# A dilated convolution with gates: the order of its first loads, and its doubled and halved weights

## The chip, the cores and the metric

The kernel runs on one core of one Trainium2 chip. The metric is the device time of one execution in microseconds (us); the median of several runs counts. A profiled execution of the same kernel gives the trace. In it the engines are PE (TensorE, matrix products; PEld its weight loads), DVE (VectorE), ACT (ScalarE), POOL (GpSimd) and SP (SyncE, which here only issues transfers).

## The reference

x has 2 batches of 16,000 steps with 256 channels, w three taps of 256 x 512, w_o 256 x 256, all bf16. The steps of the taps lie two apart and look backwards.

```python
B, T, D = x.shape
K = w.shape[0]
dil = 2
pad = (K - 1) * dil
xp = jnp.pad(x, ((0, 0), (pad, 0), (0, 0)))
h = jnp.einsum('btc,cd->btd', xp[:, pad:pad + T, :], w[0])
for i in range(1, K):
    off = pad - i * dil
    h = h + jnp.einsum('btc,cd->btd', xp[:, off:off + T, :], w[i])
f = h[..., :D].copy()
g = h[..., D:].copy()
z = jnp.tanh(f) * _sigmoid(g)
return z @ w_o
```

## The kernel before

**Tiling.** Four consecutive steps are one row; a group is up to 256 rows (1,024 steps), and the columns of a tile are rows. `xt` holds x transposed, channels on the partitions: `[128, 4, 2, rows]`, the 4 being the place in a row, the 2 the halves of the channels. `views` gives four views of it: `xc` and `yc` are places 0, 1 and 2, 3 of a row, `xp` and `yp` the same of the row before. The 512 output channels of the convolution are four blocks of 128, taken in `O_ORDER` (0, 2, 1, 3); blocks 0 and 1 go through tanh, 2 and 3 through sigmoid. A step k of the main loop is one block of one group, k = 4 x group + place in that order.

**Two ways to compute a block.** Group 0 (160 rows) is computed directly (`direct`, L236): for each tap two products (halves of the channels) into bank a (places 0, 1) and two into bank b (places 2, 3), in the order `TAPS`; for bank a, taps 0, 1, 2 read `xc`, `yp`, `xp`, for bank b `yc`, `xc`, `yp`. All later groups use four products instead of six (`products`, L217): `mm` = `xc` - `yp` with the weights `wm`, `pp` = `xc` + `yp` with `wp`, and the differences `dd` with tap 0 or tap 2. `wp` and `wm` are half of (tap 0 + tap 2) plus or minus half of tap 1 (`weights`, L141 to L144: ScalarE halves tap 1 into `wh_sb`, VectorE makes `wt_sb`, `wm_sb`, `wp_sb`). `copy_m2` (L247, ScalarE) copies the product of `mm` from bank b into `ss`; `combine` (L254, L255, VectorE) makes b = a - ss and a = a + ss; then the products of `dd` are added into both banks, and `activate` (L268, ScalarE) reads them. `gate` (L282, L286, VectorE) multiplies tanh and sigmoid, `out_mm` (L307) multiplies by w_o, `out_evict` (L326) copies the result out, and SyncE stores it.

**Queues and order.** The order on each engine is written out by hand; an engine runs its instructions in program order. Banks a and b have three buffers each, `ps_o` two. GpSimd makes most of `dd` (L192).

**Start.** VectorE clears `warm`, and TensorE runs `N_WARM[0]` = 27 products with it (L92). SyncE issues the load of x for group 0 (`xn`, L122, 320 KB), tap 0 (`w0_sb`, L126, 256 KB), the transposing load of chunk 1 (L105), `wo_sb` (L131, 128 KB) and the transposing load of chunk 2. A chunk is one group (chunks 0 and 1) or two. ScalarE issues taps 1 and 2 in one transfer (L118, 512 KB) beside its table load (L117). Chunk 0 isn't transposed by a transfer: `turn` (L155 to L163) does it on TensorE, 16 transposes, of whose four copies out of PSUM VectorE makes those for places 0, 1 (L161) and ScalarE those for places 2, 3 (L163). Six more products with `warm` follow, then the direct products of blocks k = 0, 1, 2, tap by tap. Then come the weights, `activate` for these three blocks, `pre_m` and `pre_p` for group 1 and its `dd`. The fourth block of group 0 (k = 3) and the first of group 1 (k = 4, `N_DIRECT`) are interleaved:

```python
direct(3, TAPS[:-1])
products(N_DIRECT, 2)
products(N_DIRECT, 1)
copy_m2(N_DIRECT)
direct(3, TAPS[-1:])
```

where 2 stands for `mm` with `wm`, 1 for `pp` with `wp`. The trace names all tap tiles `w_sb`.

Of the kernel before, what the change touches and what calls it, by code (L numbers as in the profile page):

```python
# [8 lines left out]
ACT = mybir.ActivationFunctionType  # L9
ALU = mybir.AluOpType  # L10
# [3 lines left out]
def kernel(  # L14
# [15 lines left out]

    nc = tc.nc
    bf16 = mybir.dt.bfloat16
    f32 = mybir.dt.float32
    B, T, D = x.shape
    K, _, D2 = w.shape
    P = 128
    assert K == 3 and D % P == 0 and D2 == 2 * D and T % 64 == 0
    CT = D // P  # L40
    NT = D // P
    RH = 16
    RG = 256
    N_WARM = (27, 6)
    O_ORDER = (0, 2, 1, 3)
    TAPS = (1, 2, 0)
    FIRST = (160,)
    LAST = (128, 128)
    TILES = ((0, 80), (80, 80))
    N_DIRECT = 4  # L50

    def sizes(first, last):
        rem = T // 4 - sum(first) - sum(last)
        assert rem >= 0
        odd = [rem % RG] if rem % RG else []
        return list(first) + [RG] * (rem // RG) + odd + list(last)
# [2 lines left out]
    groups, chunks = [], []  # L59
    for b in range(B):  # L60
        r0 = 0
        rs = sizes(FIRST if b == 0 else (), LAST if b == B - 1 else ())
        cuts = [1, 1] if b == 0 else []
        i = 0
        while i < len(rs):
            n = cuts.pop(0) if cuts else 2
            part = rs[i:i + n]
            chunks.append((b, r0, sum(part), len(groups), len(part)))
            for r in part:
                groups.append(dict(b=b, r0=r0, R=r, chunk=len(chunks) - 1, col=r0 - chunks[-1][1]))  # L70
                r0 += r
            i += n
    XW = max(c[2] for c in chunks)

    consts = ctx.enter_context(tc.tile_pool(name="consts", bufs=1))
# [13 lines left out]
    def warm_up(n):  # L89
        wps = ps_a.tile([P, 2 * RG], f32, name="a")  # L90
        for _ in range(n):
            nc.tensor.matmul(wps[:, :P], lhsT=warm[:], rhs=warm[:], start=True, stop=True)  # L92

    xts = {}

    def load_chunk(c):
# [13 lines left out]

    warm = consts.tile([P, P], bf16)
    nc.vector.memset(warm[:], 0.0)
    w0_sb = consts.tile([P, CT, D2], bf16)
    w12_sb = consts.tile([P, 2, CT, D2], bf16)
    wo_sb = consts.tile([P, NT, D], bf16)
    w_taps = [w0_sb, w12_sb[:, 0], w12_sb[:, 1]]
    nc.scalar.preload_act_table(ACT.Sigmoid)  # L117
    nc.scalar.dma_start(out=w12_sb[:], in_=w[1:3].rearrange("k (ct c) d -> c k ct d", c=P))  # L118
    warm_up(N_WARM[0])
    nx, rx = len(TILES), TILES[0][1]  # L120
    xn = consts.tile([P, nx, 4, D], bf16, name="xn")
    nc.sync.dma_start(  # L122
        out=xn[:rx], in_=x[0, 0:4 * nx * rx, :].rearrange("(i r j) c -> r i j c", i=nx, j=4)
    )
    xns = [xn[:, i] for i in range(nx)]
    nc.sync.dma_start(out=w0_sb[:], in_=w[0].rearrange("(ct c) d -> c ct d", c=P))  # L126
    ident = consts.tile([P, P], bf16)
    make_identity(nc, ident[:])
    for c in range(2):
        load_chunk(c)  # L130
    nc.sync.dma_start(out=wo_sb[:], in_=w_o.rearrange("(ct c) d -> c ct d", c=P))  # L131
    load_chunk(2)
    loaded = 3

    wh_sb = consts.tile([P, CT, D2], bf16)
    wt_sb = consts.tile([P, CT, D2], f32)
    wp_sb = consts.tile([P, CT, D2], bf16)
    wm_sb = consts.tile([P, CT, D2], bf16)

    def weights():  # L140
        nc.scalar.mul(wh_sb[:], w_taps[1], 0.5)  # L141
        nc.vector.tensor_tensor(out=wt_sb[:], in0=w_taps[0][:], in1=w_taps[2], op=ALU.add)
        for dst, op in ((wm_sb, ALU.subtract), (wp_sb, ALU.add)):
            nc.vector.scalar_tensor_tensor(  # L144
                out=dst[:], in0=wt_sb[:], scalar=0.5, in1=wh_sb[:], op0=ALU.mult, op1=op,
            )

    def turn(i):
        r0, r = TILES[i]
        for h in range(2):  # L150
            pool, tag = ((ps_o, "o_ps"), (ps_b, "b"))[i]
            tp = pool.tile([P, 2, CT, P], bf16, name="tp", tag=tag)
            for j in range(2):
                for ct in range(CT):
                    nc.tensor.transpose(  # L155
                        out=tp[:, j, ct, :r], in_=xns[i][:r, 2 * h + j, ct * P:(ct + 1) * P],
                        identity=ident[:r, :r],
                    )
            dst = xts[0][:, 2 * h:2 * h + 2, :, RH + r0:RH + r0 + r]
            if h == 0:  # L160
                nc.vector.tensor_copy(out=dst, in_=tp[:, :, :, :r])  # L161
            else:
                nc.scalar.copy(out=dst, in_=tp[:, :, :, :r])  # L163
# [7 lines left out]
    def pre_m(g):  # L171
        xp, yp, xc, yc = views(g)
        G = groups[g]
        G["m"] = m_pool.tile([P, 2, CT, RG], bf16, name="mm")
        return nc.vector.tensor_tensor(out=G["m"][:, :, :, :G["R"]], in0=xc, in1=yp, op=ALU.subtract)  # L175

    def pre_p(g):
        xp, yp, xc, yc = views(g)
        G = groups[g]
        G["p"] = p_pool.tile([P, 2, CT, RG], bf16, name="pp")  # L180
        return nc.vector.tensor_tensor(out=G["p"][:, :, :, :G["R"]], in0=xc, in1=yp, op=ALU.add)  # L181
# [19 lines left out]
    def products(k, which):  # L201
        g, oi = divmod(k, 4)
        G = groups[g]
        o = O_ORDER[oi]
        osl = slice(o * P, (o + 1) * P)
        R = G["R"]
        N = 2 * R
        if which in (1, 2):
            G["ab"[which - 1], oi] = (ps_a, ps_b)[which - 1].tile([P, 2 * RG], f32, name="ab"[which - 1])
        wmat, mv, bank, first = {  # L210
            2: (wm_sb, lambda ct: G["m"][:, :, ct, :R], "b", True),
            1: (wp_sb, lambda ct: G["p"][:, :, ct, :R], "a", True),
            3: (w_taps[0], lambda ct: G["d"][:, 2:4, ct, :R], "b", False),
            0: (w_taps[2], lambda ct: G["d"][:, 0:2, ct, :R], "a", False),
        }[which]
        for ct in range(CT):
            nc.tensor.matmul(  # L217
                G[bank, oi][:, :N], lhsT=wmat[:, ct, osl], rhs=mv(ct),
                start=first and ct == 0, stop=ct == CT - 1, skip_group_check=True,
            )  # L220

    def direct(k, taps):

        g, oi = divmod(k, 4)
        G = groups[g]
        o = O_ORDER[oi]
        osl = slice(o * P, (o + 1) * P)
        R = G["R"]
        xp, yp, xc, yc = views(g)
        for tap in taps:  # L230
            if tap == TAPS[0]:
                G["a", oi] = ps_a.tile([P, 2 * RG], f32, name="a")
                G["b", oi] = ps_b.tile([P, 2 * RG], f32, name="b")
            for bank, mv in (("a", (xc, yp, xp)[tap]), ("b", (yc, xc, yp)[tap])):
                for ct in range(CT):
                    nc.tensor.matmul(  # L236
                        G[bank, oi][:, :2 * R], lhsT=w_taps[tap][:, ct, osl], rhs=mv[:, :, ct, :],
                        start=tap == TAPS[0] and ct == 0, stop=tap == TAPS[-1] and ct == CT - 1,
                        skip_group_check=True,
                    )  # L240
# [16 lines left out]
    def activate(k):  # L257
        g, oi = divmod(k, 4)
        G = groups[g]
        R = G["R"]  # L260
        o = O_ORDER[oi]
        if oi == 0:
            G["th"] = act_pool.tile([P, NT, 4, RG], bf16, name="th")
            G["sg"] = act_pool.tile([P, NT, 4, RG], bf16, name="sg")
            G["z"] = z_pool.tile([P, NT, 4, RG], bf16, name="zz")
        dst = G["th"][:, o] if o < NT else G["sg"][:, o - NT]
        for h, bank in ((1, "b"), (0, "a")):
            nc.scalar.activation(  # L268
                out=dst[:, 2 * h:2 * h + 2, :R],
                in_=G[bank, oi][:, :2 * R].rearrange("p (q r) -> p q r", q=2),  # L270
                func=ACT.Tanh if o < NT else ACT.Sigmoid,
            )

    def gate(g, dt):
# [100 lines left out]
    todo, made = [], []  # L375
    turn(0)
    turn(1)
    warm_up(N_WARM[1])
    for tap in TAPS:
        for k in range(3):  # L380
            direct(k, (tap,))
    weights()
    for k in range(3):
        activate(k)
    pre_m(1)
    pre_p(1)
    for part in range(3):
        last = pre_d(1, part, nc.vector)
    pre_d(1, 3, nc.gpsimd, last)

    direct(3, TAPS[:-1])
    products(N_DIRECT, 2)
    products(N_DIRECT, 1)
    copy_m2(N_DIRECT)
    direct(3, TAPS[-1:])
    activate(3)
    combine(N_DIRECT)
    gate(0, 0)
    drain(0, N_DIRECT + 2, gate(0, 1))

    k = N_DIRECT + 1
    while k <= NB:
        g, oi = divmod(k, 4)
# [20 lines left out]
        last = None  # L424
        if k < NB and oi == (1 if g == 1 else 0) and g + 1 < NG:
            last = pre_m(g + 1)
        elif k < NB and oi == 2 and g + 1 < NG:
            last = pre_p(g + 1)
        elif oi == 3 and g < NG:
            last = gate(g, 0)  # L430
        elif oi == 1 and 1 < g < NG:
            last = gate(g - 1, 1)
# [42 lines left out]
```

## Time and profile before

| | us |
|---|---|
| Median of 3 runs | 285.53 |
| Lowest and highest | 285.46, 285.62 |
| The profiled execution | 285.54 |
| Span of its instructions | 283.6 |
| Issue of x, and time to landing | 0.74, 3.8 |
| Issue of taps 1 and 2, and time to landing | 0.76, 5.1 |
| Issue of tap 0, and time to landing | 1.20, 5.5 |
| First direct product | 5.99 |
| First product of the sums and differences (`wm`) | 12.00 |
| Granted TensorE clock, mean | 1.000 |

The times of instructions are counted from the start of the span; the time of an execution has 1.9 us around the span. A row of the timeline has the start, the duration, engine, line, operation, and tiles written and read; rows that follow each other are merged (x2, x27), and square brackets tell how long the engine was idle before, and what ended that. One product's duration has its way through the array in it, so that products in a row overlap: their pitch, from start to start, is shorter. "To landing" runs from the start of the issue until the whole transfer has been reported.

### The profile page before, as it was taken

To read this page: it belongs to the slowest core of one execution; us is meant where nothing else is said; L and a number is where in the kernel's file an instruction comes from. 1 tells how busy PE (TensorE), PEld (TensorE's weight loads), DVE (VectorE), ACT (ScalarE), POOL (GpSimd) and SP (SyncE) were. 2 spreads that over 40 slices of the span, in tenths; PEclk is the share of its full clock that TensorE was granted. 3 is DMA by queue.
4 is the path that set the end of the run, shared out by engine and by line. 5 is a ranking of instruction groups with operands and counts; after the bars stand their busy time and mean duration, and the time that the engine had idled before them with its cause. 6 is when DMAs were issued, how large, how long until landed. Compare 5 with 4: busy or idle time off the path is not lost.

```text
span 283.6 us, 4821 instructions
## 1 busy us (share of the span) xinstructions
PE 278.1 (98%) x1621; PEld 157.0 (55%) x1621; DVE 240.7 (85%) x403; ACT 260.3 (92%) x521; POOL 126.3 (45%) x133
## 2 busy tenths in 40 slices
PE   7999999999999999999999999999999999999994
PEld 6645555555555555555555555555555555555783
DVE  1999888888888888888888888888888888888884
ACT  4489999999999999999999999999999999999994
POOL 1145454445445544544554455445445544543430
PEclk9999999999999999999999999999999999999999
DMA  7964691732828228091461814528282341401232
GB/s 202 207 153 104 164 198 74 169 97 85 180 74 191 75 83 216 37 226 66 118 158 46 220 74 107 160 74 192 75 181 85 89 124 60 119 37 75 76 113 81
DMA packets 76039, 34.50 MB, mean 122 GB/s; under 512 B 66512, under 2 KB 68048, under 8 KB 76016
## 3 DMA queue, kind: packets, MB, share of 16 engines
q1 hardware_dynamic: 75488, 33.69, 45.1%
q10 hardware_dynamic: 528, 0.52, 0.6%
q8 instruction: 12, 0.20, 0.3%
q14 instruction: 11, 0.09, 0.1%
HBM read 1.25 MB, written 16.38 MB: 62 GB/s over the span
## 4 chain that ended last, share of the span: by engine, by line
PE 96%; DMA 2%; DVE 0%; DVEq 0%; issue 0%; ACT 0%
PE a L217 37%; PE b L217 37%; PE o_ps L307 19%; DMA w_sb<-in_w_dram 2%; PE a L236 1%; PE b L236 1%; PE a L352 0%; DVE osb_end L359 0%; PE b L352 0%; DVEq L470 0%; ACT L117 0%
## 5 line engine op out<-in xcount | busy, mean ns | idle before, releaser
L192 POOL TENSOR_TENSOR dd<-xt 128x512 bf16<-128x512 bf16 (+2 forms) x125 | 125.5, 1004 | 147.6 <-DVE zz L286 64.6
L254 DVE TENSOR_TENSOR b<-a,ss 128x512 f32<-128x512 f32 (+2 forms) x128 | 86.6, 676 | 33.1 <-ACT ss L247 31.7
L255 DVE TENSOR_TENSOR a<-a,ss 128x512 f32<-128x512 f32 (+2 forms) x128 | 85.3, 667 | 0.0
L247 ACT COPY ss<-b 128x512 f32<-128x512 f32 (+2 forms) x128 | 72.9, 569 | 12.2 <-PE b L217 0.8
L217 PEld LDWEIGHTS <-w_sb 128*128 128x128 bf16 x512 | 49.9, 98 | 56.4 <-issue 0.5
L217 PE MATMUL a<-dd,w_sb 128*128 128x512 bf16 (+2 forms) x256 | 73.8, 370 | 0.0
L217 PE MATMUL a<-pp,wp_sb 128*128 128x512 bf16 (+2 forms) x256 | 73.8, 370 | 0.0
L217 PE MATMUL b<-dd,w_sb 128*128 128x512 bf16 (+2 forms) x256 | 73.8, 370 | 0.0
L217 PE MATMUL b<-mm,wm_sb 128*128 128x512 bf16 (+2 forms) x256 | 73.8, 370 | 0.0
L307 PE MATMUL o_ps<-wo_sb,zz 128*128 128x256 bf16 x488 | 73.2, 273 | 0.0
L326 ACT CAST osb<-o_ps 128x512 bf16<-128x512 f32 x121 | 71.7, 592 | 0.0
L307 PEld LDWEIGHTS <-zz 128*128 128x128 bf16 x488 | 47.7, 98 | 29.8
L286 DVE TENSOR_TENSOR zz<-th,sg 128x1024 bf16<-128x1024 bf16 (+1 forms) x65 | 42.4, 653 | 0.0
L268 ACT ACTIVATE th<-b 128x512 bf16<-128x512 f32 (+2 forms) x66 | 39.1, 593 | 3.1 <-PE b L236 3.0
L217 PEld LDWEIGHTS <-wp_sb 128*128 128x128 bf16 x256 | 25.1, 98 | 27.9
L268 ACT ACTIVATE sg<-b 128x512 bf16<-128x512 f32 (+2 forms) x66 | 39.1, 592 | 0.9 <-PE b L217 0.5
L268 ACT ACTIVATE th<-a 128x512 bf16<-128x512 f32 (+2 forms) x66 | 39.3, 595 | 0.0
L268 ACT ACTIVATE sg<-a 128x512 bf16<-128x512 f32 (+2 forms) x66 | 39.1, 592 | 0.0
L217 PEld LDWEIGHTS <-wm_sb 128*128 128x128 bf16 x256 | 25.0, 98 | 3.4
L175 DVE TENSOR_TENSOR mm<-xt 128x1024 bf16<-128x1024 bf16 (+2 forms) x32 | 21.3, 667 | 0.0
L181 DVE TENSOR_TENSOR pp<-xt 128x1024 bf16<-128x1024 bf16 (+2 forms) x32 | 21.2, 664 | 0.0
L236 PEld LDWEIGHTS <-w_sb 128*128 128x128 bf16 x48 | 4.6, 97 | 2.4 <-DMA w_sb<-in_w_dram 0.5
(33 smaller groups left out, 36.4 us busy)
## 6 DMA issues: line engine op xcount, KB each, us to landing
out_dram<-osb SPq DMA_DIRECT2D x61, 256.0 KB, 2.0
w_sb<-in_w_dram ACTq DMA_DIRECT2D x1, 512.0 KB, 5.1
xn<-in_x_dram SPq DMA_DIRECT2D x1, 320.0 KB, 3.8
xt<-in_x_dram SPq DMA_TRANSPOSE x17, 6.4
w_sb<-in_w_dram SPq DMA_DIRECT2D x1, 256.0 KB, 5.5
out_dram<-osb_end SPq DMA_DIRECT2D x2, 128.0 KB, 1.9
wo_sb<-in_w_o_dram SPq DMA_DIRECT2D x1, 128.0 KB, 3.0
out_dram<-osb_odd SPq DMA_DIRECT2D x8, 16.0 KB, 1.5
```

What stands on the lines that cost most here:

```text
L175: return nc.vector.tensor_tensor(out=G["m"][:, :, :, :G["R"]], in0=xc, in1=yp, op=ALU.subtract)
L181: return nc.vector.tensor_tensor(out=G["p"][:, :, :, :G["R"]], in0=xc, in1=yp, op=ALU.add)
L192: ins = eng.tensor_tensor(out=G["d"][:, j, :, :R], in0=a[:, q], in1=s[:, q], op=ALU.subtract)
L217: nc.tensor.matmul(G[bank, oi][:, :N], lhsT=wmat[:, ct, osl], rhs=mv(ct), start=first and ct == 0, stop=ct == CT - 1, skip_group_check=True,)
L236: nc.tensor.matmul(G[bank, oi][:, :2 * R], lhsT=w_taps[tap][:, ct, osl], rhs=mv[:, :, ct, :], start=tap == TAPS[0] and ct == 0, stop=tap = ...
L247: nc.scalar.copy(out=G["ss", oi][:, :N], in_=G["b", oi][:, :N])
L254: nc.vector.tensor_tensor(out=pb[:, :N], in0=pa[:, :N], in1=ss[:, :N], op=ALU.subtract)
L255: nc.vector.tensor_tensor(out=pa[:, :N], in0=pa[:, :N], in1=ss[:, :N], op=ALU.add)
L268: nc.scalar.activation(out=dst[:, 2 * h:2 * h + 2, :R], in_=G[bank, oi][:, :2 * R].rearrange("p (q r) -> p q r", q=2), func=ACT.Tanh if o ...
L286: return nc.vector.tensor_tensor(out=G["z"][:, dt, :, :full], in0=G["th"][:, dt, :, :full], in1=G["sg"][:, dt, :, :full], op=ALU.mult)
L307: nc.tensor.matmul(o_ps[:, q, :], lhsT=lhsT, rhs=wo_sb[:, dt, :], start=(dt == 0), stop=(dt == NT - 1),)
L326: copy(out=osb[:, 2 * jp:2 * jp + 2, :], in_=o_ps[:])
```

## The change

The loads are put in another order. SyncE issues x, tap 2 and tap 0, then chunks 1 and 2. ScalarE issues tap 1, with a wait for the eighth warm-up product; 16 more warm-up products follow the eight, and four instead of six follow the transposes. `TAPS`, the order of the direct products, is (2, 0, 1) instead of (1, 2, 0). `wo_sb` is issued by ScalarE behind two doublings.

The weights are not halved any more: `wm` and `wp` are tap 0 + tap 2 minus or plus tap 1, the products of `dd` read doubled copies of taps 0 and 2, and the activations of all groups but the first have a scale of 0.5. `pre_m` and `pre_p` of group 1 stand before the first activations in the program (they are on VectorE, those on ScalarE). In the interleaved part, the products with `wp` and `copy_m2` change places, and the direct products of the last tap come between.

`LAST` is written differently, with the same groups as before.

```diff
-    N_WARM = (27, 6)
+    N_WARM = (8, 16, 4)
-    TAPS = (1, 2, 0)
+    TAPS = (2, 0, 1)
...
-    nc.scalar.preload_act_table(ACT.Sigmoid)
-    nc.scalar.dma_start(out=w12_sb[:], in_=w[1:3].rearrange("k (ct c) d -> c k ct d", c=P))
-    warm_up(N_WARM[0])
+    w_in = [w[k].rearrange("(ct c) d -> c ct d", c=P) for k in range(K)]
     nc.sync.dma_start(
         out=xn[:rx], in_=x[0, 0:4 * nx * rx, :].rearrange("(i r j) c -> r i j c", i=nx, j=4)
     )
-    nc.sync.dma_start(out=w0_sb[:], in_=w[0].rearrange("(ct c) d -> c ct d", c=P))
+    for k in TAPS[:2]:
+        nc.sync.dma_start(out=w_taps[k][:], in_=w_in[k])
+    nc.scalar.preload_act_table(ACT.Sigmoid)
+    begun = warm_up(N_WARM[0])
+    tc.add_manual_dep(
+        nc.scalar.dma_start(out=w_taps[TAPS[2]][:], in_=w_in[TAPS[2]]).ins, begun.ins.name,
+        mybir.DependencyInfo(mybir.DependencyClass.Sync, mybir.DependencyReason.DATA),
...
+    )
+    warm_up(N_WARM[1])
...
-    nc.sync.dma_start(out=wo_sb[:], in_=w_o.rearrange("(ct c) d -> c ct d", c=P))
...
-    def weights():
-        nc.scalar.mul(wh_sb[:], w_taps[1], 0.5)
-        nc.vector.tensor_tensor(out=wt_sb[:], in0=w_taps[0][:], in1=w_taps[2], op=ALU.add)
-        for dst, op in ((wm_sb, ALU.subtract), (wp_sb, ALU.add)):
-            nc.vector.scalar_tensor_tensor(
-                out=dst[:], in0=wt_sb[:], scalar=0.5, in1=wh_sb[:], op0=ALU.mult, op1=op,
-            )
...
-            3: (w_taps[0], lambda ct: G["d"][:, 2:4, ct, :R], "b", False),
-            0: (w_taps[2], lambda ct: G["d"][:, 0:2, ct, :R], "a", False),
+            3: (wd0_sb, lambda ct: G["d"][:, 2:4, ct, :R], "b", False),
+            0: (wd2_sb, lambda ct: G["d"][:, 0:2, ct, :R], "a", False),
...
-                func=ACT.Tanh if o < NT else ACT.Sigmoid,
+                func=ACT.Tanh if o < NT else ACT.Sigmoid, scale=1.0 if g == 0 else 0.5,
...
-    warm_up(N_WARM[1])
+    warm_up(N_WARM[2])
...
-    weights()
+    nc.scalar.mul(wd0_sb[:], w_taps[0][:], 2.0)
+    nc.scalar.mul(wd2_sb[:], w_taps[2][:], 2.0)
+    nc.scalar.dma_start(out=wo_sb[:], in_=w_o.rearrange("(ct c) d -> c ct d", c=P))
+    nc.vector.tensor_tensor(out=wt_sb[:], in0=w_taps[0][:], in1=w_taps[2][:], op=ALU.add)
+    nc.vector.tensor_tensor(out=wm_sb[:], in0=wt_sb[:], in1=w_taps[1][:], op=ALU.subtract)
+    nc.vector.tensor_tensor(out=wp_sb[:], in0=wt_sb[:], in1=w_taps[1][:], op=ALU.add)
+    pre_m(1)
+    pre_p(1)
     for k in range(3):
         activate(k)
-    pre_m(1)
-    pre_p(1)
...
     products(N_DIRECT, 2)
-    products(N_DIRECT, 1)
     copy_m2(N_DIRECT)
     direct(3, TAPS[-1:])
+    products(N_DIRECT, 1)
```

More of the change, by code (lines that the diff above doesn't have):

```diff
@@ L43 @@
     RG = 256
-    N_WARM = (27, 6)
+    N_WARM = (8, 16, 4)
     O_ORDER = (0, 2, 1, 3)
-    TAPS = (1, 2, 0)
+    TAPS = (2, 0, 1)
     FIRST = (160,)
-    LAST = (128, 128)
+    LAST = ((), (128, 128))
     TILES = ((0, 80), (80, 80))
@@ L61 @@
         r0 = 0
-        rs = sizes(FIRST if b == 0 else (), LAST if b == B - 1 else ())
+        rs = sizes(FIRST if b == 0 else (), LAST[min(b, 1)])
         cuts = [1, 1] if b == 0 else []
@@ L91, in warm_up @@
         for _ in range(n):
-            nc.tensor.matmul(wps[:, :P], lhsT=warm[:], rhs=warm[:], start=True, stop=True)
+            last = nc.tensor.matmul(wps[:, :P], lhsT=warm[:], rhs=warm[:], start=True, stop=True)
+        return last
     xts = {}
@@ L112 @@
     nc.vector.memset(warm[:], 0.0)
-    w0_sb = consts.tile([P, CT, D2], bf16)
-    w12_sb = consts.tile([P, 2, CT, D2], bf16)
+    w_taps = [consts.tile([P, CT, D2], bf16, name=f"w{k}_sb") for k in range(K)]
     wo_sb = consts.tile([P, NT, D], bf16)
-    w_taps = [w0_sb, w12_sb[:, 0], w12_sb[:, 1]]
-    nc.scalar.preload_act_table(ACT.Sigmoid)
-    nc.scalar.dma_start(out=w12_sb[:], in_=w[1:3].rearrange("k (ct c) d -> c k ct d", c=P))
-    warm_up(N_WARM[0])
     nx, rx = len(TILES), TILES[0][1]
     xn = consts.tile([P, nx, 4, D], bf16, name="xn")
+    w_in = [w[k].rearrange("(ct c) d -> c ct d", c=P) for k in range(K)]
     nc.sync.dma_start(
@@ L124 @@
     )
-    xns = [xn[:, i] for i in range(nx)]
-    nc.sync.dma_start(out=w0_sb[:], in_=w[0].rearrange("(ct c) d -> c ct d", c=P))
+    for k in TAPS[:2]:
[5 more added lines that the diff above has]
+        mybir.DependencyInfo(mybir.DependencyClass.Sync, mybir.DependencyReason.DATA),
+        reason="the third tap leaves the transfer rate to the rows and the first two taps",
+    )
+    warm_up(N_WARM[1])
     ident = consts.tile([P, P], bf16)
@@ L130 @@
         load_chunk(c)
-    nc.sync.dma_start(out=wo_sb[:], in_=w_o.rearrange("(ct c) d -> c ct d", c=P))
     load_chunk(2)
     loaded = 3
-    wh_sb = consts.tile([P, CT, D2], bf16)
+    wd0_sb = consts.tile([P, CT, D2], bf16)
+    wd2_sb = consts.tile([P, CT, D2], bf16)
     wt_sb = consts.tile([P, CT, D2], f32)
@@ L155, in turn @@
                     nc.tensor.transpose(
-                        out=tp[:, j, ct, :r], in_=xns[i][:r, 2 * h + j, ct * P:(ct + 1) * P],
+                        out=tp[:, j, ct, :r], in_=xn[:r, i, 2 * h + j, ct * P:(ct + 1) * P],
                         identity=ident[:r, :r],
```

## The prediction, made before the changed kernel was run

> **What bounds the kernel now.** I read the page first, for the engine that never rests, then the chain of waits, then TensorE's own rows at the start, then the transfers of the first 8 us by queue, and last the rows around the first sums of VectorE.
>
> ```profile
> PE 278.1 (98%) x1621; PEld 157.0 (55%) x1621; DVE 240.7 (85%) x403; ACT 260.3 (92%) x521; POOL 126.3 (45%) x133
> ...
> PE 96%; DMA 2%; DVE 0%; DVEq 0%; issue 0%; ACT 0%
> ```
>
> TensorE is busy for 98% of the span, and the chain that ended last is 96% TensorE and 2% one transfer. So a change counts if it alters when TensorE's stream of real products begins, or puts a hole into it. The change leaves their number as it is; only the warm-up products go from 33 to 28, all before the stream begins.
>
> ```profile
> 0.99 3.03 PE L92 MATMUL a<-warm 128*128 128x128 bf16 x27 [0.99 <-DVE warm L112]
> 4.59 0.75 PE L155 MATMUL tp<-ident,xn 80*128 80x80 bf16 x16 [0.57 <-DMA xn<-in_x_dram]
> 5.17 0.50 PE L92 MATMUL a<-warm 128*128 128x128 bf16 x6
> ...
> 4.95 0.61 DVE L161 COPY xt<-tp 128x320 bf16<-128x320 bf16 x2 [4.01 <-PE tp L155]
> 5.09 0.75 ACT L163 COPY xt<-tp 128x320 bf16<-128x320 bf16 x2 [3.07 <-PE tp L155]
> ...
> 5.99 0.43 PE L236 MATMUL a<-xt,w_sb 128*128 128x320 bf16 x2 [0.31 <-DMA w_sb<-in_w_dram]
> ```
>
> The columns are start, duration, engine and line. x lands at 0.74 + 3.8 = 4.54 (issue and time to landing), the transposes follow at 4.59, and the copies out of PSUM end at 4.95 + 0.61 = 5.56 on VectorE and 5.09 + 0.75 = 5.84 on ScalarE. The stream begins at 5.99, when taps 1 and 2 have landed (0.76 + 5.13 = 5.89). The rows were ready 0.05 us before: both paths are nearly critical, and speeding up the taps alone would give nothing.
>
> Next the packets by queue; q1 is SyncE's, q10 ScalarE's; the columns are packets, MB, share of 16 engines. In order, the stretches are 1.7 to 3.1 (one line), 3.1 to 3.7 (two), 3.7 to 4.8 (two) and 4.8 to 5.5 us (two).
>
> ```profile
> q1 hardware_dynamic: 135, 0.28, 83.6%
> ...
> q10 hardware_dynamic: 104, 0.11, 63.3%
> q1 hardware_dynamic: 40, 0.05, 27.3%
> ...
> q10 hardware_dynamic: 347, 0.36, 109.3%
> q1 hardware_dynamic: 1, 0.00, 0.2%
> ...
> q1 hardware_dynamic: 173, 0.18, 78.0%
> q10 hardware_dynamic: 77, 0.06, 31.7%
> ```
>
> The loads go nearly one after another in the order of issue, across both queues: x (0.74) until 3.7, taps 1 and 2 (0.76) from 3.1 to 5.4, tap 0 (1.20) from 4.8. The 512 KB on the other queue hardly shared time with x.
>
> **The change, step by step.** S is the start of the stream; it was 5.99.
>
> *Landing of x.* It stays first. Only its last 40 packets (3.1 to 3.7) ran beside the other queue; at the rate of the stretch before (135 in 1.4 us) they take 0.41 us instead of 0.6. So x lands 0 to 0.2 us earlier; I take 0.1, between the ends: 4.45.
>
> *Order of the taps.* Tap 2 comes first, and its products into bank a read `xp`, which VectorE's copies fill; ScalarE's copies are read only by bank b, two products (0.27 us) later. Tap 1's products into bank a read `yp`, ScalarE's. VectorE's copies end 5.56 - 4.54 = 1.02 us after the landing, ScalarE's 1.30. With 0.06 for the semaphore (4.54 to 4.59, 5.89 to 5.96), S = 4.45 + 1.02 + 0.06 = 5.53, and bank b at 5.81 just fits its copies (4.45 + 1.36 = 5.81). The warm-up products behind the transposes go from six to four, and end before. Tap 2 must be there by 5.47: its 256 packets follow x at about 3.6 and need 0.8 us (as tap 0's, from 4.8 to about 5.6), and x's lag from last packet to landing was 0.85: 5.25. The other bound is that it lands as the 512 KB did, at 5.89, and S stays at 5.96. I take 5.53: -0.46 us.
>
> *Taps 0 and 1.* Tap 0 takes the place of the second half of the 512 KB, so about 5.9; TensorE asks for it 12 products after S. The pitch is 0.1365 us (22 pairs from 5.99 to 11.99), so at 7.17. Tap 1 waits for the eighth warm-up product: 27 in 3.03 us, the last 0.31 long, is a pitch of 0.105, so 0.99 + 7 x 0.105 + 0.31 = 2.04. Behind that wait on ScalarE stand only the copies of 5.09. Tap 1's place in the row of transfers is tap 0's of before (6.7), unless the transposing loads are ahead; TensorE wants it at S + 24 x 0.1365 = 8.8, VectorE at 7.2.
>
> *SyncE's queue.* It issues one more tap (0.42 + 0.06) ahead of chunk 1 and no `wo_sb` (0.58 + 0.04) between chunks 1 and 2: chunk 1 goes from 1.68 to 2.16, chunk 2 from 7.21 to about 7.1. Chunk 1 landed at 1.68 + 6.9 = 8.58, so 9.06 at worst; `pre_m(1)` wants it at 9.57. `wo_sb` goes out behind the doublings at about 6 and lands 3.0 us later, or 5 behind transposes; its first use was at 17.17. Both cost nothing.
>
> *Weights and activations.* VectorE keeps three operations of 1.22 to 1.23 us; the two that lose their scalar lie between 0.69 (a bf16 row of that size) and 1.23, I take 1.22. The chain from `wt_sb` to the last `dd` took 12.76 - 6.84 = 5.92, so it ends at 5.96 + 5.92 = 11.9, with nothing on the path. ScalarE has two doublings instead of one halving, 2 x 1.06, from 5.96 to 8.1; the first activation can start only at S + 28 x 0.1365 + 0.17 = 9.5, so the idle time there (3.04 us before) covers them; a tap 0 later than 7.3 would uncover them. A scale of 0.5 instead of none: the activations take 592 to 595 ns, the copies of that shape 569; 24 ns either way on 264 activations is 6.3 us, within ScalarE's idle 23.3. I take nothing.
>
> *The order around the first sums.* Here is the loss.
>
> ```profile
> 12.63 0.59 ACT L247 COPY ss<-b 128x512 f32<-128x512 f32 x1 [0.53 <-PE b L217]
> ...
> 13.25 0.70 DVE L254 TENSOR_TENSOR b<-a,ss 128x512 f32<-128x512 f32 x1 [0.49 <-ACT ss L247]
> ...
> 13.86 0.69 DVE L255 TENSOR_TENSOR a<-a,ss 128x512 f32<-128x512 f32 x1
> ...
> 14.70 0.59 PE L217 MATMUL a<-dd,w_sb 128*128 128x512 bf16 x2
> ...
> 16.14 0.59 PE L217 MATMUL b<-dd,w_sb 128*128 128x512 bf16 x2
> 16.74 0.59 PE L217 MATMUL a<-dd,w_sb 128*128 128x512 bf16 x2
> ```
>
> VectorE idled until `ss` came at 13.22, then worked without a gap to the second pair of sums, for which TensorE waited (16.14 instead of 15.99, 16.74 instead of 16.57). Before, the sums could start at S + 7.26. Now `wp`'s products stand behind four products of the last tap: they start at S + 6.01 + 0.43 + 0.55 = S + 6.99, end 0.59 later, and the sums start at S + 7.61, with `ss` there at S + 7.23. All that follows on VectorE, the gates and the second sums, moves by 0.35 us against S, and so do the products that wait for it. TensorE makes nothing of this up later, for it has no idle time. The bounds are 0 (a gate or a sum with slack that I don't see) and 0.35; I take 0.35, as VectorE's row has no gap.
>
> **Sum.** -0.46 + 0.35 = -0.11 us. The profiled execution took 285.54 us (span 283.6 and 1.9 around it; the median of the runs is 285.53): 285.43.
>
> **Two rules weighed.** The Trainium skill's page "DMA: Bandwidth & Descriptors", section "Issuing engines are not separate DMA queues", says that loads from several engines interleave on the same 16 DMA engines. By it the 512 KB would have held x up by about half of its 2.0 us, x would now land near 3.6, S would be tap 2's 5.31 and the sum 285.2; the rows above, with q10's first packets after 3.1, speak against it. Its page "TensorE: Matmul & The Clock Gate", Part 1, says that the clock doubles after a busy window of some 3.4 us that runs freely; 24 products of 0.105 us are shorter, and so were 27, after which the clock was up. By the page the stream could start at half clock, the second rival's time.
>
> **The rivals.**
>
> *The clock comes up late (slower).* The warm-up products ran at 0.105 us each at first, and the six at 5.17 at (0.50 - 0.22)/5 = 0.056: the clock had doubled by 4.59, with 3.03 us of products before. Now there are 24, until 3.7, and then a gap of 0.8 us instead of 0.57. Should 2.7 us not suffice, transposes (16 x 0.07 instead of 0.037) and four products of 0.105 bring S to about 6.05, and the clock doubles only some 2.9 us after 4.5, at 7.4: 1.35 us at half speed lose 0.68. That is 6.05 + 0.68 - 5.53 = 1.2 us: 286.6. It decides if the doubling hasn't come when the transposes start. For it: the count is cut; against: 2.7 us is 90% of 3.03.
>
> *Tap 1 behind the transposes (slower).* SyncE begins to issue chunk 1 at 2.16, ScalarE tap 1 at 2.1, which is a draw. Behind all of chunk 1, whose packets ended at 8.0, tap 1 would land near 9.65; `mm` would be ready 2.97 later plus 0.07 (8.17 to 11.14 before), and TensorE stand 1.2 us: 286.6. It costs from 8.4 on. Against it: issuing chunk 1 took 4.86 us, so most of it comes after tap 1.
>
> *The start gains more (faster).* If x lands early enough that only tap 2 counts, S is 5.31, and if the later sums find slack: 285.54 - 0.68 = 284.86. For it: x's lag of 0.85 us is long; against: its packets began at 1.7 and ran alone to 3.1.
>
> **Numbers.** Forecast 50%, its own range 285.3 to 285.9 (tap 2 late at the upper end); late clock 20%; tap 1 late 14%; more gain 16%. What a measurement can tell from no change is 0.2%, 0.57 us: faster means below 284.96, slower above 286.10. Faster: 13 of the last 16. Slower: 20 and 9 of the 14. The same: the remaining 58. Range: 284.8 to 286.8, to the ends of the rivals, with 0.2 more above, where two of them lie.
>
> **What would show it.** Right: x landing at 4.4 to 4.5, first product near 5.5, transposes at a pitch of 0.037 us, the first sum 7.6 us after S behind `wp`'s products, and no wait for taps 0 and 1. Wrong: transposes and first products at double length; a wait for `w_sb` in the middle of the direct products; first sums at S + 7.3; or a difference that grows after 20 us, which would be the activations.

## The result and the profile after

The changed kernel took 287.06 us (median of 22 executions, 285.17 to 288.09), the kernel before beside it 285.50 (22 executions, 285.19 to 287.57). The ratio of the means is 1.0038, 95% interval 1.0021 to 1.0056: slower by more than the 0.2% named in the prediction, and its median lies above the forecast range. The median hides the shape. The 22 executions are two lots (groups of times) with nothing between them: a short one, 8 from 285.17 to 285.73 us (median 285.32), and a long one, 14 from 286.93 to 288.09. Of the 22 of the kernel before one was long (287.57); the median of the others is 285.47.

The first profile of the changed kernel is of the short lot (285.62 us, span 283.6). From its page, the busy times and the chain by engine:

```profile
PE 278.1 (98%) x1616; PEld 156.4 (55%) x1616; DVE 240.8 (85%) x403; ACT 261.3 (92%) x522; POOL 126.1 (44%) x133
...
PE 96%; DMA 1%; DVE 1%; issue 0%; DVEq 0%
```

TensorE is the bound as before, and ScalarE's second doubling has only filled idle time (261.3 instead of 260.3 us). The timeline of the same execution, in order: the products that warm up, the transposes, the warm-up products behind them, the first direct products, tap 0's arrival at TensorE and at VectorE, `dd`, the products with `wp`, the first sums, and the first product with w_o.

```profile
0.99 2.74 PE L93 MATMUL a<-warm 128*128 128x128 bf16 x24 [0.99 <-DVE warm L114]
...
4.44 0.75 PE L153 MATMUL tp<-ident,xn 80*128 80x80 bf16 x16 [0.71 <-DMA xn<-in_x_dram]
...
5.02 0.39 PE L93 MATMUL a<-warm 128*128 128x128 bf16 x4
...
5.55 0.43 PE L234 MATMUL a<-xt,w_sb 128*128 128x320 bf16 x2
...
7.26 4.21 PEld L234 LDWEIGHTS <-w_sb 128*128 128x128 bf16 x32 [0.24 <-DMA w_sb<-in_w_dram]
...
7.32 1.23 DVE L383 TENSOR_TENSOR wt_sb<-w_sb 128x1024 f32<-128x1024 bf16 x1 [1.91 <-DMA w_sb<-in_w_dram]
...
12.07 1.10 DVE L190 TENSOR_TENSOR dd<-xt 128x512 bf16<-128x512 bf16 x3
...
12.62 0.59 PE L215 MATMUL a<-pp,wp_sb 128*128 128x512 bf16 x2
...
13.32 0.70 DVE L252 TENSOR_TENSOR b<-a,ss 128x512 f32<-128x512 f32 x1 [0.15 <-ACT sg L266]
...
17.24 0.60 PE L305 MATMUL o_ps<-wo_sb,zz 128*128 128x256 bf16 x4
```

In the kernel before, the first product with w_o is this row:

```profile
17.17 0.60 PE L307 MATMUL o_ps<-wo_sb,zz 128*128 128x256 bf16 x4
```

The stream starts at 5.55 instead of 5.99, but the first product with w_o comes at 17.24 instead of 17.17: the 0.44 us gained have been given back, and 0.07 more, by then. From that product on nothing differs: 283.6 - 17.24 = 266.4 us to the end of the span, and 283.6 - 17.17 = 266.4 before. So in an execution of the short lot the scale of the activations costs nothing visible, and all of the change happens in the first 17 us.

### The profile page after: what moved, and what is told of

Read it like the earlier page. It is cut to its first block, busy times and chain, and to the rows that moved or that the text cites. A ratio compares the mean times of both kernels' runs of the same rounds, so it can differ in the third digit from the quotient of the medians.

```text
span 283.6 us, 4814 instructions
## 1 busy us (share of the span) xinstructions
PE 278.1 (98%) x1616; PEld 156.4 (55%) x1616; DVE 240.8 (85%) x403; ACT 261.3 (92%) x522; POOL 126.1 (44%) x133
## 3 DMA queue, kind: packets, MB, share of 16 engines
HBM read 1.25 MB, written 16.38 MB: 62 GB/s over the span
## 4 chain that ended last, share of the span: by engine, by line
PE 96%; DMA 1%; DVE 1%; issue 0%; DVEq 0%
PE a L215 37%; PE b L215 37%; PE o_ps L305 19%; DMA xn<-in_x_dram 1%; PE a L234 1%; PE b L234 1%; DVE b L252 0%; DVE zz L284 0%; DVE xt L159 0%; PE a L350 0%; DVE osb_end L357 0%; DVE zo L280 0%; PE b L350 0%; DVEq L473 0%; PE tp L153 0%
## 5 line engine op out<-in xcount | busy, mean ns | idle before, releaser
L215 PEld LDWEIGHTS <-wd_sb 128*128 128x128 bf16 x512 | 49.8, 98 | 56.9 <-issue 0.9
L215 PE MATMUL b<-dd,wd_sb 128*128 128x512 bf16 (+2 forms) x256 | 73.8, 370 | 0.1
L215 PE MATMUL a<-dd,wd_sb 128*128 128x512 bf16 (+2 forms) x256 | 73.8, 370 | 0.0
L234 PEld LDWEIGHTS <-w_sb 128*128 128x128 bf16 x48 | 4.5, 97 | 2.4 <-issue 0.3
```

The source lines that it names most:

```text
L215: nc.tensor.matmul(G[bank, oi][:, :N], lhsT=wmat[:, ct, osl], rhs=mv(ct), start=first and ct == 0, stop=ct == CT - 1, skip_group_check=True,)
L234: nc.tensor.matmul(G[bank, oi][:, :2 * R], lhsT=w_taps[tap][:, ct, osl], rhs=mv[:, :, ct, :], start=tap == TAPS[0] and ct == 0, stop=tap = ...
```

## The experiments

The runs are named e1 to e12; each changes the kernel before or the changed kernel by the edit shown.

**A profile of the long lot.** The question that the lots put is which of the two slower rivals makes the long one: the clock that comes up late, or tap 1 behind the transposing loads. The first run is the changed kernel unchanged.

> The changed kernel once more, for a second profile, because its 22 executions fall into two lots (8 from 285.2 to 285.7 us, 14 from 286.9 to 288.1 us) and the profile at hand is of the fast lot. If the clock comes up late in the slow lot (theory), a profile of that lot shows the transposes and the first direct products at twice their pitch (0.07 and 0.27 us instead of 0.037 and 0.137), with the loads landing as in the fast one. If tap 1 lands behind the transposing loads (rival), the products have their normal pitch, and a wait for w_sb of 1.5 to 2.5 us stands before the 25th direct product. If the execution is of the fast lot, about 285.5 us, it tells nothing.

It took 287.56 us, a long one. TensorE's rows of its timeline:

```profile
0.98 2.74 PE L93 MATMUL a<-warm 128*128 128x128 bf16 x24 [0.98 <-DVE warm L114]
4.22 1.25 PE L153 MATMUL tp<-ident,xn 80*128 80x80 bf16 x16 [0.49 <-DMA xn<-in_x_dram]
5.26 0.63 PE L93 MATMUL a<-warm 128*128 128x128 bf16 x4
5.71 0.72 PE L234 MATMUL a<-xt,w_sb 128*128 128x320 bf16 x2
6.22 0.74 PE L234 MATMUL b<-xt,w_sb 128*128 128x320 bf16 x2
...
8.89 0.74 PE L234 MATMUL a<-xt,w_sb 128*128 128x320 bf16 x2
9.42 0.49 PE L234 MATMUL b<-xt,w_sb 128*128 128x320 bf16 x2
9.74 0.43 PE L234 MATMUL a<-xt,w_sb 128*128 128x320 bf16 x2
10.01 0.43 PE L234 MATMUL b<-xt,w_sb 128*128 128x320 bf16 x2
```

There is no wait for a tap. The transposes take 1.25 us instead of 0.75, though x landed earlier, and a pair of direct products comes every 0.53 us until about 9.5, then every 0.27. The account closes: the start at 5.71 instead of 5.55 is 0.16 us, the first 14 products at 0.265 instead of 0.137 are 1.8, together 2.0; the first product with w_o comes at 19.16 instead of 17.24, and this execution is 287.56 - 285.62 = 1.9 us longer than the one of the short lot. Only TensorE is slow: VectorE's `wt_sb` (1.23 us) and ScalarE's first doubling (1.06 us) last as long as in the short execution. All of TensorE's work runs at about half its pace and then, at about 9.5, at its usual one; this is what is called the clock that comes up late here, read from the pitch (what the column for the clock says stands in the last section).

**24 products in the kernel before, 27 in the changed one, and no wait for tap 1.**

```diff
# e2, kernel before
-    N_WARM = (27, 6)
+    N_WARM = (24, 6)
# e3, changed kernel
-    N_WARM = (8, 16, 4)
+    N_WARM = (8, 19, 4)
# e4, changed kernel
-    tc.add_manual_dep(
-        nc.scalar.dma_start(out=w_taps[TAPS[2]][:], in_=w_in[TAPS[2]]).ins, begun.ins.name,
...
-    )
+    nc.scalar.dma_start(out=w_taps[TAPS[2]][:], in_=w_in[TAPS[2]])
```

> The kernel before with 24 instead of 27 warm-up products ahead of the transposes; loads and order untouched. Theory (too few products, then a gap: the clock comes up late): executions some 1.5 to 2.5 us longer become common, near 287.3, beside some at 285.5. Rival (tap 1 behind the transposes): nothing changes, all at 285.5, because here no tap can fall behind them.

> The changed kernel with 27 instead of 24 products ahead of the transposes (8, 19, 4), all else as it is. Theory: nearly all executions at 285.2 to 285.7, as the products now last as long as in the kernel before, and the long ones are as rare as there (1 in 22). Rival: the two lots stay as they are, a median near 287.

> The changed kernel with tap 1 issued at once by ScalarE, without the wait for the eighth product, so that it can't fall behind a transposing load. Rival: one lot only, 285.2 to 286. Theory: the two lots stay, with long executions of 287 to 288 in more than a third of the runs.

With 24 products the kernel before has the two lots too: 7 of 12 executions from 286.94 to 287.69 us, 5 from 285.19 to 285.38 (ratio 1.0027, 1.0003 to 1.0052). With 27 products the changed kernel has lost its long lot: 12 executions from 285.22 to 286.21, median 285.64, ratio to the kernel before 0.9996 (0.9977 to 1.0015); five of the 12 lie above the 285.7 that was expected. Without the wait for tap 1 the lots stay: 8 of 12 from 286.84 to 288.0 (ratio 1.0042, 1.0020 to 1.0065). The profile of e2 is of a long execution (287.34 us) and shows the same half pace in the kernel before, until about 9.5 too:

```profile
4.24 1.25 PE L155 MATMUL tp<-ident,xn 80*128 80x80 bf16 x16 [0.51 <-DMA xn<-in_x_dram]
...
6.58 0.74 PE L236 MATMUL b<-xt,w_sb 128*128 128x320 bf16 x2
7.11 0.74 PE L236 MATMUL a<-xt,w_sb 128*128 128x320 bf16 x2
...
9.71 0.44 PE L236 MATMUL b<-xt,w_sb 128*128 128x320 bf16 x2
9.99 0.44 PE L236 MATMUL a<-xt,w_sb 128*128 128x320 bf16 x2
```

So the three products decide how often a long execution comes, in either kernel, and tap 1's place among the transfers doesn't; the rival falls. What these runs don't separate: three more products are more work, and they also shorten the idle time ahead of the transposes. The length of that idle time alone doesn't sort the four profiles with 24 products: it was 0.71 us in the first profile of the changed kernel and 0.38 in e4's, both short executions, and 0.49 and 0.51 in e1's and e2's, both long.

In the profile of e4 tap 1 goes ahead of tap 2, and the stream starts at 5.75 instead of 5.55, with a wait for a tap. Its four short executions have 285.66 in the middle against 285.32; four are too few to price that.

**Twelve and thirty-four products in the kernel before.** The edits are `N_WARM = (12, 6)` and `(34, 6)`.

> The kernel before with 12 instead of 27 warm-up products, 1.6 us of them, then a gap until x lands. Theory (the clock rises only at the end of a stretch in which TensorE was busy long enough, wherever that stretch lies): no execution below 286, most of them 0.7 to 2.5 us longer than 285.6, the first direct products at a pitch of 0.27 us. Rival (only products right before the transposes count, the six behind them suffice): all at 285.6 to 286.

> The kernel before with 34 instead of 27 products. Theory: no execution longer than 286.2 (with 27 it was 1 in 22), median 285.3 to 285.7: the start of the stream hangs on taps 1 and 2 and not on the transposes, so that the later transposes cost at most 0.2 us. Rival (more products only delay): median 285.8 or more.

With 12, six executions lie between 286.22 and 287.62, none at 285.5 (ratio 1.0054, 1.0038 to 1.0069), and the first direct products have the pitch of 0.27 us: as expected. With 34, none of 12 is above 286.45, while 7 of the 23 of the kernel before beside them were above 287.5. But the median rose to 286.02, which the rival expected. In its profile (286.27 us) the 34 products keep the transposes until 4.59 us (they start at 4.10 in e6, with 27), the stream starts at 6.47, and the clock still rises only in the first direct products:

```profile
0.99 3.81 PE L92 MATMUL a<-warm 128*128 128x128 bf16 x34 [0.99 <-DVE warm L112]
4.59 1.27 PE L155 MATMUL tp<-ident,xn 80*128 80x80 bf16 x16
...
6.47 0.65 PE L236 MATMUL a<-xt,w_sb 128*128 128x320 bf16 x2
6.96 0.43 PE L236 MATMUL b<-xt,w_sb 128*128 128x320 bf16 x2
```

The ratio, 0.9998 (0.9975 to 1.0020), is even only because of the long executions on the other side.

**The place of wp's products.** In e6 the kernel before gets the changed order; in e5 the changed kernel, with 27 products, gets the old one.

```diff
# e6, kernel before; e5 is the reverse
     products(N_DIRECT, 2)
-    products(N_DIRECT, 1)
     copy_m2(N_DIRECT)
     direct(3, TAPS[-1:])
+    products(N_DIRECT, 1)
```

> The kernel before with only that move: the products with wp behind the four last direct products. If the move costs 0.35 us by itself, the median is 285.95, the first sums start at 13.6 instead of 13.25 us, and the third and fourth products of the second block follow as much later. Rival: there is slack behind the first sums, and the time stays at 285.6.

> The changed kernel with 27 products ahead of the transposes, and the products with wp again before copy_m2 and the last direct products, as in the kernel before. If the move of those products costs what the prediction said (first sums 0.35 us later against the start of the stream), this is 0.3 to 0.4 us shorter than the run with 27 products and the changed order (285.64), near 285.3, and the first sums start about 7.3 us after the first direct product. Rival: the late landing of tap 0 sets the sums anyway (VectorE still busy with dd), then at most 0.1 us shorter, and TensorE waits for VectorE before wp's products.

e6 took 285.95 us against 285.48 (11 and 29 executions, ratio 1.0020, 1.0011 to 1.0029). VectorE's rows of its timeline at the first sums, and TensorE's row with `wp`:

```profile
11.24 1.10 DVE L192 TENSOR_TENSOR dd<-xt 128x512 bf16<-128x512 bf16 x3
...
12.94 0.59 PE L217 MATMUL a<-pp,wp_sb 128*128 128x512 bf16 x2
...
13.65 0.70 DVE L254 TENSOR_TENSOR b<-a,ss 128x512 f32<-128x512 f32 x1 [1.31 <-ACT sg L268]
```

VectorE was done with `dd` at 12.34 and idled for 1.31 us; the sums start at 13.65 instead of 13.25, and the first product with w_o at 17.56 instead of 17.17. The row names a ScalarE activation, `sg`, as the releaser. It can't be that one: in the kernel before the same sums start at 13.25, ahead of `sg`:

```profile
13.61 0.44 ACT L268 ACTIVATE sg<-b 128x320 bf16<-128x320 f32 x1 [0.39 <-PE b L236]
```

What the sums read and what came last is `wp`'s products, which end at 12.94 + 0.59 = 13.53. e5 took 285.26 us, 0.38 less than with the changed order (e3, 285.64). The two were measured at different times; against the kernel before beside each, e3 is even with it (285.64) and e5 is 0.22 us below (285.48; ratio 0.9993, 0.9984 to 1.0001). In the rows the move shows more plainly: the first sums start 7.84 us after the stream in e3 (13.48 and 5.64) and 7.40 in e5. e5's rows:

```profile
7.16 1.23 DVE L383 TENSOR_TENSOR wt_sb<-w_sb 128x1024 f32<-128x1024 bf16 x1 [1.78 <-DMA w_sb<-in_w_dram]
...
11.91 1.10 DVE L190 TENSOR_TENSOR dd<-xt 128x512 bf16<-128x512 bf16 x3
12.31 0.59 ACT L245 COPY ss<-b 128x512 f32<-128x512 f32 x1 [0.53 <-PE b L215]
...
12.93 0.70 DVE L252 TENSOR_TENSOR b<-a,ss 128x512 f32<-128x512 f32 x1
```

Here the sums follow `dd` with no gap: once `wp`'s products are early, the chain that begins with tap 0 sets them too. But `ss` ends at 12.31 + 0.59 = 12.90, and in the kernel before the sums started 0.03 after `ss`; so the two chains end together in this profile. The landing of tap 0 is a candidate for the next term, no more.

**Tap 0 earlier.** e8 is e5 without the wait for tap 1 (the edit of e4); e12 is e8 again, e11 has 29 products and e9 34 (`N_WARM` = (8, 21, 4) and (8, 26, 4)).

> The changed kernel with 27 products, the old place of wp's products, and tap 1 issued without a wait: tap 0 then lands near 6.4 instead of 7.2 us, tap 2 at 5.7. If the late tap 0 is what is left of a loss, this is 0.1 to 0.2 us shorter than the same kernel with the wait; if the start of the stream (5.75 instead of 5.55) counts for more, it is 0.1 to 0.2 us longer.

> The same with 27 products once more, beside other executions of the kernel before. If the gain of the first time (285.05 against 285.48) is real, 0.3 to 0.6 us below the short executions of the kernel before, and few or no executions above 286.5. If it was the chip of that time, the same as the kernel before.

> The kernel with tap 1 unwaited and the old place of wp's products, with 29 products ahead of the transposes. They end near 4.2 us, where x lands at 4.0 to 4.4, so that they delay the transposes by at most 0.2 us. Theory: the median lies at 285.0 to 285.25, with no execution above 286.5. If even two more products delay by all of their 0.21 us, 285.25 to 285.35.

> The kernel with tap 1 unwaited and the old place of wp's products, now with 34 products ahead of the transposes, which last until x has landed. In its profile with 27 the clock rose only in the direct products (three at about twice their pitch, some 0.35 us). If the clock is what is left, the clock is up before the direct products in nearly all executions, the spread shrinks, and the median falls by 0 to 0.3 us, to 284.8 to 285.05. Rival: the seven products delay the transposes by more than the clock brings: 285.2 to 285.5.

e8 took 285.05 us, e5 beside it 285.26, the kernel before 285.48; the ratio of e8 to that is 0.9988 (0.9979 to 0.9996). The repetition gave 285.08 against 285.51 (0.9984, 0.9968 to 0.9999), 29 products 285.11 (0.9987, 0.9978 to 0.9996). This version beats the kernel before three times, in the medians by 0.4 us; that is less than the 0.2% that the prediction named, but all three intervals lie below 1. It is 2.0 us below the median of the changed kernel, which was measured at another time, and none of its 33 executions with 27 or 29 products was long. With 34 it took 285.60, above even what the rival expected: in its profile the transposes start at 4.59 and last 1.27 us, and the stream starts at 6.11. Which part of the version brings the 0.4 us isn't shown: the 0.21 between e5 and e8 isn't clear of the spread of their 11 executions each (284.85 to 285.77 and 284.86 to 285.62). The profile of e12 (285.07 us) has the clock up at the transposes, and its gain is still there at the first product with w_o, 16.68 instead of 17.17:

```profile
5.49 0.45 PE L230 MATMUL a<-xt,w_sb 128*128 128x320 bf16 x2 [0.40 <-DMA w_sb<-in_w_dram]
...
16.68 0.60 PE L301 MATMUL o_ps<-wo_sb,zz 128*128 128x256 bf16 x4
```

VectorE's rows of e8:

```profile
6.36 1.23 DVE L379 TENSOR_TENSOR wt_sb<-w_sb 128x1024 f32<-128x1024 bf16 x1 [0.97 <-DMA w_sb<-in_w_dram]
...
11.11 1.09 DVE L186 TENSOR_TENSOR dd<-xt 128x512 bf16<-128x512 bf16 x3
13.13 0.70 DVE L248 TENSOR_TENSOR b<-a,ss 128x512 f32<-128x512 f32 x1 [0.92 <-ACT ss L241]
```

Tap 0 is there 0.8 us sooner than in e5, `dd` ends at 12.20, and the sums wait for `ss` once more, as in the kernel before: the products set them, 7.6 us after the start at 5.53 here, because this execution's first three products ran at the slow pitch.

**All executions by the number of products ahead of the transposes** (over 286.6 us is long):

| Products | Kernels | Executions | Long |
|---|---|---|---|
| 12 | e7 | 6 | 5, the sixth 286.22 |
| 24 | changed, e1, e2, e4 | 47 | 30 |
| 27 | before (all that were measured) | 124 | 11 |
| 27 | e3, e5, e6, e8, e12 | 56 | 0 |
| 29 | e11 | 11 | 0 |
| 34 | e9, e10 | 24 | 0, but 0.5 us later in the median |

The 11 of the kernel before came unevenly: 7 among 23 executions measured together, none among 29 others. So how often a long execution comes isn't a fixed share of a kernel. None of the 11 was profiled; that they too are the late clock is likely from their times, and not shown.

## Why the prediction was wrong, by its steps

*Landing of x and start of the stream.* Right: x landed at 0.74 + 3.7 = 4.4 (forecast 4.45), tap 2 in time, and the stream started at 5.55 (5.53), tap 2's first products with VectorE's copies alone (they started before ScalarE's copies ended, at 4.94 + 0.75 = 5.69). That x came 0.1 us earlier is partly luck: its landing wanders by more than that between executions of one order, 4.5 in the profile of the kernel before and 4.1 in that with 12 products (e7).

*Taps 0 and 1.* Tap 1 came in time, as forecast; tap 0's landing had the wrong size. Tap 0 was put at 5.9, in the place of the second half of the 512 KB; it landed at about 7.2, where `wt_sb` and TensorE's weight load waited for it (7.32 and 7.26). That cost TensorE 0.07 us against its pitch and moved the chain of `wt_sb` to `dd` to 13.17 instead of 11.9, 0.15 us before the sums. It is covered in the changed order, and level with `ss` in e5. It wanders, too: `wt_sb` starts at 7.32, 7.00, 6.70 and 7.16 in the profiled executions with the wait for tap 1 (the changed kernel twice, e3, e5), and from 6.36 to 6.60 in the five without it (e4, e8, e9, e11, e12), where tap 1 goes first. All are later than the 5.96 of the forecast. Why tap 0 lands this late wasn't tried by itself.

*Order around the first sums.* The mechanism was right and the size a little low: put at 0.35 us, measured alone 0.40 in the rows (13.65 against 13.25) and 0.47 in the medians. In the changed kernel the sums started 7.77 us after S (forecast 7.61, before 7.26), so the loss was 0.51. Of the 0.16 more, `wp`'s products began 0.08 later against S, 0.07 of it the wait for tap 0; and the sums began 0.11 us after the end of these products (12.62 + 0.59 = 13.21), where the forecast took the 0.03 that rows show behind `ss`.

*SyncE's queue, weights, activations.* Right: no wait for `wo_sb` or chunk 1, and 266.4 us behind the first product with w_o in both. The two doublings were covered, but only just: as tap 0 was late they ran from 7.24 instead of 5.96, and ScalarE idled for 0.41 us before its first activation, at 9.65 (forecast 9.5).

*The sum.* -0.11 us was forecast. In the profile's rows it is -0.44 + 0.51 = +0.07 at the first product with w_o, and the two profiled executions differ by +0.08. The medians of the short lots, picked out after the fact, differ by -0.15 (285.32 against 285.47), and with 27 products (e3) the changed kernel is even with the kernel before (285.64 both). So without the long lot the change is worth about nothing; whether it is a little below nothing, as forecast, these runs can't tell.

*The clock.* This is the step that failed, in its chance and in its price. The sum put a late clock at nothing; it was a rival with 20% (the first in its list, though its paragraph on the rules calls it the second), argued down with "2.7 us is 90% of 3.03". A long execution came 14 times in 22, and so it is the median. What the step took for a sum of busy time has an edge between 24 and 27 products: 30 of 47 executions long, against 11 of 180. And the price, 1.2 us, assumed that the clock rises some 2.9 us after the transposes begin, at 7.4. In the two profiles of long executions (e1, e2) it rose at about 9.5, 5.3 us after the transposes began; in e1 the half pace of the direct products alone cost 1.8 us where the forecast had 0.68, and the long lot lies 1.4 to 2.6 us above 285.5, in the middle 2.0. The prediction had one profile of the kernel before and none that showed how near its 27 products were to the edge; the 3 times shown were all short. The Trainium skill's "TensorE: Matmul & The Clock Gate", Part 1, has the half clock, says that the window runs freely and that the moment differs from run to run; the prediction weighed this rule and set it aside, because 27 products, shorter than its 3.4 us, had sufficed. The runs side with the page in the main thing: the same kernel has its clock up by 4.44 us in one execution and at 9.5 in another. The page gives the spread as 500 ns either way, though; these two, with an idle stretch ahead of the transposes in each, lie 5 us apart, and the measurement decides.

## What to carry to other kernels

Warm-up work ahead of a load can decide the result, as three products of 0.1 us each did here: when a load is moved, count how long TensorE works before its first real product and how long it then idles, and try the number of products by itself, with enough executions to see two lots. A median between or within two lots is no sum of terms; separate the lots first. And where a start is advanced, follow the next chain (here `wp`'s products and `dd`, to the first sums) to the point from which both kernels run alike, since a gain at the start is real only if it is still there.

## What the hardware showed unexpectedly

The moment at which the clock rises, read from the pitch of the products, was by 4.44 us, during the transposes (e4, which took 0.98 us) or at 9.5 with 24 products, before the transposes or near 6 with 27, by 4.29 with 29, and near 7.5 with 12. Even 34 products, busy without a gap from 0.99 to 4.80 us, left the transposes of e9 and e10 slow (1.27 us instead of 0.75), and in e10 the first direct products too, until 6.9. The column for the granted clock doesn't show this. In the stretches of the long execution (its bounds and length, TensorE's busy time, products in it, granted clock, share and rate of the transfers), TensorE works on 13 products in the 3 us from 6 to 9, and on 17 of the same size in the 2 us from 10 to 12, with a clock of 1.00 in both:

```profile
6.00:9.00 3.00, 3.00 (x13) 1.00 1.18 209
10.00:12.00 2.00, 2.00 (x17) 1.00 1.10 240
```

What exactly TensorE must do, and for how long, to have its clock raised isn't settled by these runs.
